# Second MLP, first wide chunk: second layer in seven products, residual rows parked in DRAM, g applied at PSUM

## Chip, cores and metric

The kernel runs on one NeuronCore of a Trainium2 chip. The metric is device time in microseconds (us) of one launch, as the median of several runs. One execution was also taken by the hardware profiler; all rows below come from it.

## What is computed

Attention with a window of 128 keys, a first MLP over tokens and channels ("moe"), and a second MLP ("moe2"); the change touches the second MLP:

```python
def _moe2_ref(x, g_ln, w_ch1, w_ch2):          # x: 4 x 576 x 512, w_ch1: 512 x 2048, w_ch2: 2048 x 512
    mu = np.mean(x, axis=-1, keepdims=True)
    var = np.mean((x - mu) ** 2, axis=-1, keepdims=True)
    xn = (x - mu) / np.sqrt(var + 1e-06) * g_ln
    ch = np.maximum(xn @ w_ch1, 0.0) @ w_ch2
    return (x + ch).astype(np.float32)
```

The 4 x 576 tokens are 18 tiles of 128 rows. float32 accuracy comes from splitting each operand in a high and a low float32r part and adding three products (high-high, high-low, low-high).

## The kernel before

Both MLPs run over three chunks of tokens: a wide one (tiles 0 to 7), a small one (tiles 16, 17) and a wide one (tiles 8 to 15). `steps` lists them as (layer, chunk, tiles, n); layer 1 is the second MLP and has n = 0 to 7 in each chunk, a step taking two blocks of 128 of the 2048 hidden columns. The text calls step n of the second MLP's first wide chunk "1a step n", and that of its second wide chunk "1b step n"; the first MLP's chunks are 0a and 0b.

In a wide chunk the first layer (`seven_products`, lines 1138 to 1140) multiplies 2 x 2 blocks in seven products instead of eight, each of 6 matmuls of 512 columns. Its ends go through `relu_to` (969, 971), which writes the hidden tile's high part on ACT and its low part on DVE. The second layer of step n is spread between the first-layer products of step n + 1. In 1a it is `second` (lines 1236 to 1259): for each of the 8 token tiles 6 matmuls of 512 columns (1251 to 1253), and one DVE addition to the residual `u` (1256). In 1b, steps 0 to 6, it is `second_fast` (1261): seven products for each of two pairs of tiles, of 6 matmuls of 256 columns each (1288), with one copy of a bank to another on ACT (1302) and twelve DVE additions of 512 elements a step (1307). This form needs sums of hidden blocks, which `parts_of` makes at the end of the first layer (1194 to 1203, with splits in high and low on ACT at 385 and on POOL or DVE at 403 or 401), and sums of weight blocks t1 to t4. Those are made once, during 1a, by `keep_sums`: per step eight POOL subtractions of 128 columns and two splits; the results go to DRAM as `ds1nh`, `ds1nl`, and `sums_of` reads them in 1b.

Weights arrive as float64 and are converted by five instructions a block (`load_f64`: ACT 449, DVE 452, 454, 456, 464). `stage_w` converts blocks ahead of their use and keeps them in DRAM (`d`), `load_w` reads them back or converts on the spot. `STAGE_RATES` says how many blocks a step stages, and in the attention stage `W_START` and `W_STEP` place conversions. For blocks of the second MLP's first weight, `convert_w` multiplies by the layer norm's gain g (516, POOL or DVE).

The residual `u` is one SBUF tile of 18 x 512 columns. The order of all engines' instructions is made at build time: every operation carries costs and dependencies, and `Plan.order` lists them by need; engines then run their lists in order.

## Time and profile before

| | |
|---|---|
| median of 3 runs | 834.96 us (833.67 to 835.32) |
| profiled execution | 835.53 us |
| its span, first to last instruction | 833.8 us |
| PE busy | 821.5 us, 99% |
| DVE busy | 659.1 us, 79% |
| POOL busy | 466.9 us, 56% |
| ACT busy | 428.5 us, 51% |

The busy share of PE is the share of the span in which some matmul is under way. The stage of interest, 1a, runs from 448.8 to 611.5 us of the span; 1b's steps from 661.5 us.

### The profile page before, as it was taken

The numbers are of one execution on the slowest core, as the hardware profiler recorded it, in microseconds if no ns is written. First come the engines' busy times: TensorE is split into PE (matmuls) and PEld (weight loads), VectorE is DVE, ScalarE is ACT, GpSimd is POOL, SyncE is SP. The second block draws the span as 40 slices with busy tenths as digits, with TensorE's granted clock in tenths as the row PEclk, the third lists the DMA queues.
The fourth block names the chain that finished last, engine by engine and source line by source line (L and its number), as shares of the span: only waits on it lengthen the run. The fifth ranks groups of instructions, "written<-read, shape, count | busy, mean of one in ns | idle before, by whom it ended". The sixth has DMA issues, their size and how long they took to land.

```text
span 833.8 us, 14352 instructions
## 1 busy us (share of the span) xinstructions
PE 821.5 (99%) x4732; PEld 693.4 (83%) x4732; DVE 659.1 (79%) x1379; ACT 428.5 (51%) x1015; POOL 466.9 (56%) x723
## 2 busy tenths in 40 slices
PE   8999999999999999999999999999999999999998
PEld 6777788888888898888888888888889889999996
DVE  5888777978787989987889868989666767777785
ACT  5888677643344535334368333447456634444430
POOL 2785466756354567544248666857533656666640
PEclk9999999999999999999999999999999999999999
DMA  9679645454678899987861544888977663443302
GB/s 328 191 184 306 232 140 191 143 186 144 216 226 297 293 317 322 339 293 240 280 238 54 188 154 139 290 309 300 354 263 237 226 226 130 137 141 116 102 26 101
DMA packets 80474, 179.21 MB, mean 215 GB/s; under 512 B 9104, under 2 KB 10768, under 8 KB 80400
## 3 DMA queue, kind: packets, MB, share of 16 engines
q1 hardware_dynamic: 79920, 176.98, 62.9%
q0 software_dynamic: 480, 1.31, 0.7%
q8 instruction: 37, 0.61, 0.3%
q14 instruction: 37, 0.30, 0.1%
HBM read 138.15 MB, written 38.80 MB: 212 GB/s over the span
## 4 chain that ended last, share of the span: by engine, by line
PE 92%; DVE 4%; ACT 3%; DMA 1%; issue 1%; POOL 0%; DVEq 0%; ACTq 0%; POOLq 0%
PE tok L1253 10%; PE tok L1251 10%; PE b L1138 10%; PE tok L1252 10%; PE b L1139 10%; PE b L1140 10%; PE tok L1288 5%; PE p L1288 4%; PE ps_s L636 3%; PE ps_v L648 3%; PE p L891 2%; PE b L482 2%; PE b L481 2%; PE b L480 2%; PE ps_t L693 1%; ACT pr L686 1%
## 5 line engine op out<-in xcount | busy, mean ns | idle before, releaser
L1256 DVE TENSOR_TENSOR u<-tok,u 128x512 f32<-128x512 f32 x196 | 134.4, 687 | 52.5 <-PE tok L1253 51.1
L1251 PE MATMUL tok<-w2h,hh 128*128 128x512 f32 x392 | 154.0, 393 | 0.0
L1253 PE MATMUL tok<-w2h,hl 128*128 128x512 f32 x392 | 152.9, 390 | 0.2 <-DVE hl L971 0.2
L1252 PE MATMUL tok<-w2l,hh 128*128 128x512 f32 x392 | 152.8, 390 | 0.0
L1138 PE MATMUL b<-xh,w1h 128*128 128x512 f32 x384 | 150.4, 392 | 0.3 <-DVE b L401 0.3
L1139 PE MATMUL b<-xl,w1h 128*128 128x512 f32 x384 | 149.8, 390 | 0.0
L1140 PE MATMUL b<-xh,w1l 128*128 128x512 f32 x384 | 149.6, 389 | 0.0
L403 POOL TENSOR_TENSOR w1l<-w,w1h 128x256 fp32r<-128x256 f32 (+1 forms) x112 | 78.9, 726 | 111.4 <-ACT w1h L385 103.4
L969 ACT ACTIVATE hh<-b 128x512 fp32r<-128x512 f32 (+1 forms) x112 | 58.7, 542 | 136.8 <-PE b L1140 95.5
L1253 PEld LDWEIGHTS tok<-w2h,hl 128*128 128x128 f32 x392 | 73.6, 188 | 16.4 <-DVE hl L971 0.8
L1251 PEld LDWEIGHTS tok<-w2h,hh 128*128 128x128 f32 x392 | 73.7, 188 | 15.1 <-DVE u L1256 0.8
L971 DVE SCALAR_TENSOR_TENSOR hl<-b,hh 128x512 fp32r<-128x512 f32 (+1 forms) x112 | 67.2, 617 | 23.9 <-ACT hh L969 23.2
L1252 PEld LDWEIGHTS tok<-w2l,hh 128*128 128x128 f32 x392 | 73.7, 188 | 14.3
L1140 PEld LDWEIGHTS b<-xh,w1l 128*128 128x128 f32 x384 | 72.1, 188 | 15.4
L1138 PEld LDWEIGHTS b<-xh,w1h 128*128 128x128 f32 x384 | 72.2, 188 | 14.6 <-DVE b L401 0.7
L1139 PEld LDWEIGHTS b<-xl,w1h 128*128 128x128 f32 x384 | 72.2, 188 | 13.5
L449 ACT ACTIVATE e<-rh 128x512 bf16<-128x512 bf16 (+2 forms) x62 | 39.7, 641 | 69.4 <-DMA rh<-wb 22.2
L403 POOL TENSOR_TENSOR w1l<-st,w1h 128x256 fp32r<-128x256 f32 x58 | 44.9, 795 | 47.9 <-ACT w1h L385 42.0
L686 ACT ACTIVATE pr<-t,mn 128x128 f32<-128x128 f32 x144 | 55.8, 391 | 14.1 <-DVE mn L677 14.0
L704 POOL TENSOR_SCALAR_AFFINE_SELECT pf<-pf 128x512 f32<-128x512 f32 x64 | 42.1, 659 | 34.6 <-ACT pf L385 28.3
L401 DVE TENSOR_TENSOR b<-b,p 128x512 f32<-128x512 f32 x56 | 38.9, 695 | 20.1 <-PE b L1140 19.5
L403 POOL TENSOR_TENSOR xl<-st,xh 128x256 fp32r<-128x256 f32 x48 | 39.0, 834 | 21.0 <-ACT xh L385 16.6
(193 smaller groups left out, 1919.9 us busy)
## 6 DMA issues: line engine op xcount, KB each, us to landing
w<-d SPq DMA_DIRECT2D x86, 256.0 KB, 4.2
rw<-wb SPq DMA_DIRECT2D x32, 512.0 KB, 5.4
rh<-wb SPq DMA_DIRECT2D x32, 512.0 KB, 5.2
rw<-wa SPq DMA_DIRECT2D x24, 512.0 KB, 4.3
rh<-wa SPq DMA_DIRECT2D x24, 512.0 KB, 4.3
d<-y SPq DMA_DIRECT2D x30, 256.0 KB, 5.3
keys<-kT SPq DMA_DIRECT2D x18, 256.0 KB, 4.6
q<-qT SPq DMA_DIRECT2D x18, 256.0 KB, 4.9
```

Of the source, the lines that this page charges most:

```text
L403: ENGINE[e].tensor_tensor(get()[:, c], ga()[:, c], gb()[:, c], alu)
L686: op({"ACT": 580}, lambda m=m: nc.scalar.activation(out=pr.t[:, m], in_=t.t[:, m], func=AF.Exp, bias=mn.t[:, m:m + 1], scale=-1.0, accum_o ...
L969: op({"ACT": act(n, True)}, lambda: nc.scalar.activation(out=hh.t[:, c], in_=go(), func=AF.Relu), [o], [(hh, key)])
L971: mark[0] = op({"DVE": dve(n)}, lambda: nc.vector.scalar_tensor_tensor(out=hl.t[:, c], in0=go(), scalar=0.0, in1=hh.t[:, c].bitcast(F32), ...
L1138: nc.tensor.matmul(g.t, wh.t[:, w], xh.t, start=start and k == 0, stop=False, skip_group_check=True)
L1139: nc.tensor.matmul(g.t, wh.t[:, w], xl.t, start=False, stop=False, skip_group_check=True)
L1140: nc.tensor.matmul(g.t, wl.t[:, w], xh.t, start=False, stop=stop and k == 1, skip_group_check=True)
L1251: nc.tensor.matmul(o.t, hh.t[:, c:c + P], wh.t, start=j == 0, stop=False)
L1252: nc.tensor.matmul(o.t, hh.t[:, c:c + P], wl.t, start=False, stop=False)
L1253: nc.tensor.matmul(o.t, hl.t[:, c:c + P], wh.t, start=False, stop=j == 1)
L1256: op({"DVE": dve(DM)}, lambda o=o, i=i: nc.vector.tensor_tensor(u[i].t, o.t, u[i].t, ALU.add), [o], [u[i]])
L1288: nc.tensor.matmul(o.t[:, p], x()[:, c], y(), start=start and p == 0 and k == 0, stop=stop and p == 1 and k == 2, skip_group_check=True)
```

## The change

1. `FAST2` now also names 1a, steps 1 to 6: their second layer runs as `second_fast`, their first layer ends in `parts_of`.
2. The sums t1 to t4 are needed in the step that makes them. `keep_sums` writes them into new row buffers: raw sums in `f` (one buffer), high and low parts in `r` (four). They still go to DRAM for 1b. Step 0 keeps the old places (`few`).
3. To make room, `u` becomes nine pairs of tiles. The pairs of tiles 8 to 17 live in the buffers `r` and `f`; `put_away` writes them to DRAM when 1a begins (10 DMAs of 256 KB), and `bring_back` reads them at 1a step 7 (10 more). All layer norm statistics of tiles 8 to 15 are now due ahead of that.
4. g is no longer multiplied into the weights. The second MLP's transposed inputs are scaled as they leave PSUM: on ACT by a per-partition scale, on DVE by `scalar_tensor_tensor` in place of `tensor_tensor`.
5. Conversions: from n = 22 on the attention stage has one at every n instead of every second; 0a stages one block a step (before none), 0b three (before two).

```diff
-STAGE_RATES = {(0, 2): 2, (1, 0): 2}
+STAGE_RATES = {(0, 0): 1, (0, 2): 3, (1, 0): 2}
+RESTING, SUMS = range(8, 18), 8
-FAST2 = ((1, 2),)
+FAST2 = {(1, 2): range(7), (1, 0): range(1, 7)}
...
+def pair_of_rows(j):
+    if j == SUMS:
+        pairs[j] = buf("rows", [P, 2, DM], F32, "f", 1)
+    elif 2 * j in RESTING:
+        pairs[j] = buf("rows", [P, 2, DM], F32, "r", len(RESTING) // 2 - 1)
+    else:
+        pairs[j] = buf("big", [P, 2, DM], F32, "u", (NTILE - len(RESTING)) // 2)
+    u[2 * j:2 * j + 2] = [Part(pairs[j], lambda t, k=k: t[:, k]) for k in range(2)]
...
-                if W_START <= n < 2 * NTILE - 4 and (n - W_START) % W_STEP == 0:
+                if W_START <= n < 2 * NTILE - 4 and ((n - W_START) % W_STEP == 0 or n >= W_DENSE):
...
+    def copy_x(dst, get, b, gb, f):
+        if f is None:
+            return copy(dst, get, b, gb, CW, ("ACT",), True)
+        op({"ACT": act(CW, True, 1)}, lambda: nc.scalar.activation(
+            out=get(), in_=gb(), func=AF.Copy, scale=g_sb.t[:, f]), [b, g_sb], [dst])
+    def less(dst, get, b, gb, a, ga, f):
+        if f is None:
+            return minus(dst, get, b, gb, a, ga, CW, ("DVE",))
+        op({"DVE": dve(CW)}, lambda: nc.vector.scalar_tensor_tensor(
+            out=get(), in0=gb(), scalar=g_sb.t[:, f], in1=ga(), op0=ALU.mult, op1=ALU.subtract), [b, g_sb, a], [dst])
...
-        if c == 0 and (layer, 2) in FAST2 and n < (NF1, NF2)[layer] // 2 - 1:
-            keep_sums(layer, n, wtiles[used[0] - 2:used[0]], last)
-        return sums_of(layer, n, out) if fast2(s) else out
+        if c == 0:
+            if n not in FAST2.get((layer, 2), ()):
+                return out
+            places = in_rows() if fast2(s) else in_few()
+            full = in_sums() if fast2(s) else None
+            keep_sums(layer, n, wtiles[used[0] - 2:used[0]], last, *places, full)
+            return with_sums(out, *quarters(*places)) if fast2(s) else out
+        return with_sums(out, *sums_of(layer, n)) if fast2(s) else out
...
+    def put_away(tiles):
+        for i in tiles:
+            d = resting[i] = buf("dram", [P, DM], F32, f"r{i}")
+            op({"DMA": 728}, lambda x=u[i], d=d: nc.sync.dma_start(out=d.t, in_=x.t), [u[i]], [d])
+    def bring_back(tiles):
+        for i in tiles:
+            if i % 2 == 0:
+                pair_of_rows(i // 2)
+            op({"DMA": 728}, lambda x=u[i], d=resting[i]: nc.sync.dma_start(out=x.t, in_=d.t), [resting[i]], [u[i]])
...
+            if (layer, c) == (1, 0):
+                while todo:
+                    do_next()
+                put_away(RESTING)
+        if (layer, c) == (1, 0) and n == NF2 // 2 - 1:
+            bring_back(RESTING)
```

How the built order moves, at three places. PE in 1a, where the second layer of step 1 begins: `b` is a first-layer product, `tok` and `p` are second-layer banks. Before:

```order
L1138 MATMUL b_6281<-xh_5835,w1h 128x512
L1139 MATMUL b_6281<-xl_5846,w1h 128x512
L1140 MATMUL b_6281<-xh_5835,w1l 128x512
L1251 MATMUL tok<-w2h,hh 128x512
L1252 MATMUL tok<-w2l,hh 128x512
L1253 MATMUL tok<-w2h,hl 128x512
```

Now:

```order
L1356 MATMUL tok<-w2h,hl 128x256
L1368 MATMUL p_6357<-hh 128x512
L1206 MATMUL b_6360<-xh_5559,w1h 128x512
L1207 MATMUL b_6360<-xl_5573,w1h 128x512
L1208 MATMUL b_6360<-xh_5559,w1l 128x512
L1206 MATMUL b_6360<-xh_5831,w1h 128x512
L1207 MATMUL b_6360<-xl_5837,w1h 128x512
L1208 MATMUL b_6360<-xh_5831,w1l 128x512
L1356 MATMUL tok<-r,fewh 128x256 x2
L1356 MATMUL tok<-r,fewl 128x256
```

A step's 48 second-layer matmuls of 512 columns are 84 of 256; some of them read the sums in `r` that POOL has just made, and line 1368 is one extra matmul that opens a bank (two in all of 1a).

DVE in the same stretch: additions to the residual, `hl` the hidden low parts, `s`, `m`, `y` the conversion of weights. Before:

```order
L1256 TENSOR_TENSOR u<-tok,u 128x512 x2
L401 TENSOR_TENSOR b_2516<-b_2448,p_6309 128x512
L1256 TENSOR_TENSOR u<-tok,u 128x512 x2
L401 TENSOR_TENSOR b_6281<-b_2448,p_6309 128x512
L1256 TENSOR_TENSOR u<-tok,u 128x512
L401 TENSOR_TENSOR st<-w 128x256
L1256 TENSOR_TENSOR u<-tok,u 128x512
```

Now:

```order
L1266 SCALAR_TENSOR_TENSOR hl<-b_6360,hh 128x512
L1376 TENSOR_TENSOR u<-tok,u 128x2x256
L467 TENSOR_SCALAR s<-e 128x256
L1421 TENSOR_TENSOR rstd<-r_6279,y 128x8
L469 SCALAR_TENSOR_TENSOR s<-e,s 128x256
L416 TENSOR_TENSOR b_2534<-b_2465,p_6483 128x512
L479 SCALAR_TENSOR_TENSOR y<-m,s 128x512
L1376 TENSOR_TENSOR u<-tok,u 128x2x256
L1376 TENSOR_TENSOR u<-p_6357,u 128x2x256
L467 TENSOR_SCALAR s<-e 128x256
L416 TENSOR_TENSOR b_6456<-b_2465,p_6483 128x512
L1376 TENSOR_TENSOR u<-p_6392,u 128x2x256
```

Twelve additions a step stand where eight stood, between conversions and first-layer sums. In the whole order DVE has 72 additions of line 1376 more and 48 of line 1324 (1256 before) fewer; 24 hidden low parts of `relu_to` give way to 18 + 18 instructions of `parts_of`, and DVE takes 9 more low parts `hl<-st`, `fewl<-st` and 2 more sums `st<-st`. POOL takes 30 more halves of such low parts and 8 of such sums.

SP, which issues the DMAs, around the end of 1a step 6: `w` is a weight block, `ds` sums for 1b, `r_...` a parked residual tile. Before:

```order
L1114 DMA rw<-ds10h 128x1024
L1114 DMA rh<-ds10l 128x1024
L1114 DMA rw<-ds11h 128x1024
L1114 DMA y<-ds11l 128x512 x2
L1096 DMA ds16l<-fewh 128x512 x2
L524 DMA d_7523<-w 128x512
L1096 DMA ds16h<-fewl 128x512 x2
```

Now:

```order
L1179 DMA rw<-ds10h 128x1024
L1179 DMA rh<-ds10l 128x1024
L528 DMA d_7773<-y 128x512
L1133 DMA r<-r_5890 128x512
L1133 DMA r<-r_5922 128x512
L1133 DMA r<-r_5953 128x512
L1133 DMA r<-r_5986 128x512
L1161 DMA ds16h<-r 128x512
L1161 DMA ds16l<-r 128x512
L1161 DMA ds16h<-r 128x512
L1133 DMA f<-r_4797 128x512
L1133 DMA f<-r_4802 128x512
```

Ten returns like these stand in the queue; the first four wait until step 5's sums have been used, and the writes of step 6's sums and the next weight loads stand behind them.

## Rows read from the trace of the kernel before

**Rows 1.** The page: busy us (share of span) and instructions by engine.
```profile
PE 821.5 (99%) x4732; PEld 693.4 (83%) x4732; DVE 659.1 (79%) x1379; ACT 428.5 (51%) x1015; POOL 466.9 (56%) x723
```
**Rows 2.** Windows of 1a steps 2 to 6: busy us (instructions) by engine, clock, DMA.
```profile
core 0: us, PE busy (x) PEld busy (x) DVE busy (x) ACT busy (x) POOL busy (x), PEclk, DMA share, GB/s
...
487.60:508.00 20.40, 20.40 (x92) 16.89 (x91) 12.59 (x20) 7.53 (x14) 12.03 (x20) 1.00 0.37 123
508.00:528.60 20.60, 20.60 (x92) 16.84 (x91) 17.61 (x29) 9.19 (x17) 18.74 (x28) 1.00 0.61 204
528.60:549.40 20.80, 20.64 (x91) 16.78 (x90) 19.64 (x31) 8.90 (x17) 17.99 (x28) 1.00 0.89 322
549.40:569.80 20.40, 20.40 (x91) 16.89 (x90) 17.91 (x29) 8.07 (x15) 10.01 (x15) 1.00 0.81 283
569.80:590.20 20.40, 20.40 (x91) 16.89 (x90) 17.90 (x30) 14.71 (x32) 16.33 (x24) 1.00 0.90 295
```
**Rows 3.** The same view: all of 1a, small chunk after it, four steps of 1b.
```profile
448.80:611.50 162.70, 162.54 (x721) 134.02 (x722) 133.59 (x223) 74.76 (x146) 109.26 (x165) 1.00 0.67 230
611.50:661.50 50.00, 50.00 (x327) 45.56 (x327) 32.30 (x57) 32.04 (x72) 21.46 (x30) 1.00 0.79 267
701.20:779.50 78.30, 78.30 (x506) 71.23 (x505) 58.88 (x93) 36.62 (x68) 51.27 (x81) 1.00 0.40 129
```
**Rows 4.** Timeline of PE at a step's border in 1b: start us, length us.
```profile
700.93 0.28 PE L1288 MATMUL tok<-w2l,hh 128*128 128x256 f32 x1
701.05 0.28 PE L1288 MATMUL tok<-w2h,hl 128*128 128x256 f32 x1
701.17 0.40 PE L1138 MATMUL b<-xh,w1h 128*128 128x512 f32 x1
701.40 0.40 PE L1139 MATMUL b<-xl,w1h 128*128 128x512 f32 x1
```
**Rows 5.** Timeline of PE in 1a step 4, around its wait.
```profile
531.96 0.39 PE L1251 MATMUL tok<-w2h,hh 128*128 128x512 f32 x1
532.19 0.39 PE L1252 MATMUL tok<-w2l,hh 128*128 128x512 f32 x1
532.73 0.50 PE L1253 MATMUL tok<-w2h,hl 128*128 128x512 f32 x1 [0.16 <-DVE hl L971]
```
**Rows 6.** Timeline of DVE in the same step.
```profile
542.06 1.05 DVE L464 SCALAR_TENSOR_TENSOR y<-m,s 128x512 f32<-128x512 uint32 x1
543.03 0.68 DVE L1256 TENSOR_TENSOR u<-tok,u 128x512 f32<-128x512 f32 x1
543.64 0.41 DVE L456 TENSOR_SCALAR m<-rw 128x512 uint32<-128x512 uint32 x1
```
**Rows 7.** Groups by form, DVE in 1a: busy us, mean ns; idle before.
```profile
L1256 DVE TENSOR_TENSOR u<-tok,u 128x512 f32<-128x512 f32 x64 | 43.8, 686 | 15.7 <-PE tok L1253 15.3
L464 DVE SCALAR_TENSOR_TENSOR y<-m,s 128x512 f32<-128x512 uint32 x12 | 11.4, 949 | 1.0 <-POOL w L516 0.9
L456 DVE TENSOR_SCALAR m<-rw 128x512 uint32<-128x512 uint32 x11 | 7.4, 676 | 0.0
L516 DVE TENSOR_TENSOR w<-y,g_sb 128x512 f32<-128x512 f32 x3 | 3.2, 1083 | 0.0
```
**Rows 8.** Groups by form, POOL in 1a and (second row) in 1b.
```profile
L516 POOL TENSOR_TENSOR w<-y,g_sb 128x512 f32<-128x512 f32 x3 | 3.7, 1247 | 0.0
...
L403 POOL TENSOR_TENSOR fewl<-st,fewh 128x256 fp32r<-128x256 f32 x26 | 18.7, 752 | 3.7 <-PE tok L1288 3.0 <-ACT fewh L385 0.7
```
**Rows 9.** Windows of 0b: its first step, and all of it.
```profile
319.30:340.70 21.40, 21.08 (x94) 16.89 (x93) 20.50 (x38) 10.13 (x18) 17.82 (x28) 1.00 0.97 346
...
319.30:448.80 129.50, 129.18 (x584) 106.26 (x582) 111.05 (x204) 62.61 (x127) 64.54 (x101) 1.00 0.78 267
```
**Rows 10.** Groups by form, DVE in 0b.
```profile
L464 DVE SCALAR_TENSOR_TENSOR y<-m,s 128x512 f32<-128x512 uint32 x16 | 11.2, 702 | 0.2
L456 DVE TENSOR_SCALAR m<-rw 128x512 uint32<-128x512 uint32 x16 | 8.8, 553 | 0.8 <-DMA rw<-wb 0.7
```
**Rows 11.** DMA of 1a steps 6 and 7 (569.8 to 611.5): totals, one issue line.
```profile
DMA packets 6000, 12.34 MB, mean 296 GB/s; under 512 B 672, under 2 KB 672, under 8 KB 5997
...
q1 hardware_dynamic: 5997, 12.30, 85.2%
...
w<-d SPq DMA_DIRECT2D x12, 256.0 KB, 4.2
```
**Rows 12.** Waits in 1a: who waited for whom, us in total, times, longest.
```profile
ACT w2h L385 <- DMA w<-d: 16.5, 6, 5.8
```

More of the change, by code (lines that the diff above doesn't have):

```diff
@@ L113, in __init__ @@
         self.plan, self.pool, self.spec = whole.plan, whole.pool, whole.spec
-        self.ops, self.track, self.after, self.behind, self.first = [], {}, [], None, set()
+        self.ops, self.track, self.after, self.behind, self.first = [], {}, whole.after, whole.behind, set()
         self.whole, self.get = whole, get
@@ L170, in op @@
                     behind.add(b.behind.ops[0])
-                assert not getattr(b, "closed", False), f"{b.spec[2]} is used after its place was given away"
+                assert not getattr(getattr(b, "whole", b), "closed", False), f"{b.spec[2]} is used after its place was given away"
                 assert write or any(w for key2, (w, _) in b.track.items() if key is None or key2 in (None, key)), \
@@ L350, in open_pool @@
         pl.pools[name] = tc.alloc_tile_pool(name=name, **{"bufs": 1, **kw})
-    for name in ("const", "big", "wa", "raw", "cvt", "small", "hid"):
+    for name in ("const", "big", "rows", "wa", "raw", "cvt", "small", "hid"):
         open_pool(name)
@@ L372, in block_kernel @@
     after = buf("const", [P, P], F32, "after")
-    u_all = buf("big", [P, NTILE, DM], F32, "u")
-    u = [Part(u_all, lambda t, i=i: t[:, i]) for i in range(NTILE)]
+    pairs, u = [None] * (NTILE // 2), [None] * NTILE
+    def pair_of_rows(j):
[6 more added lines that the diff above has]
+        u[2 * j:2 * j + 2] = [Part(pairs[j], lambda t, k=k: t[:, k]) for k in range(2)]
+    for j in range(NTILE // 2):
+        pair_of_rows(j)
     def load(dst, get, nbytes, src):
@@ L877, in turned @@
         b = buf("psm", [P, CW], F32, f"p{turn[0]}")
-        get = [lambda i=i, k=k: u[i].t[:, k * P:(k + 1) * P] for i, k in places]
+        get = [lambda x=u[i], k=k: x.t[:, k * P:(k + 1) * P] for i, k in places]
         xs = [u[i] for i, _ in places]
@@ L1034, in fast2 @@
         layer, c, _, n = steps[s]
-        return (layer, c) in FAST2 and n < (NF1, NF2)[layer] // 2 - 1
+        return n in FAST2.get((layer, c), ())
     def w2_of(s):
@@ L1060, in keep_sums @@
+    def keep_sums(layer, n, w, last, lo, hi, full=None):
         x0, x1 = w
-        places = few()
         d = {p: buf("dram", [P, 2 * DM], F32, f"ds{layer}{n}{p}") for p in "hl"}
-        def all_of(k):
-            return places[0], lambda: places[0].t.bitcast(F32)[:, k, :DM]
+        if full is None:
+            full = [(x, lambda get=get: get().bitcast(F32)) for x, get in lo]
         def part(c):
-            return (places[0], c // 2), lambda: places[0].t.bitcast(F32)[:, c // 2, c % 2 * HW:(c % 2 + 1) * HW]
+            (x, k), get = full[c // 2]
+            return (x, k), lambda: get()[:, c % 2 * HW:(c % 2 + 1) * HW]
@@ L1454, in block_kernel @@
         pl.emit()
-    for n in ("mlq", "mlr", "mlp", "even", "psc", "pst", "psm", "hid", "small", "cvt", "raw", "wa", "big", "const", "dram"):
+    for n in ("mlq", "mlr", "mlp", "even", "psc", "pst", "psm", "hid", "small", "cvt", "raw", "wa", "rows", "big", "const", "dram"):
         pl.pools[n].release()
```

133 lines of the change are left out of this document (77 added, 56 removed).

## The prediction

> **What bounds the kernel now.** I read the page first: PE is busy 99% of the span, DVE 79%, POOL 56% [rows 1]. So time is PE's instruction stream, and the change has to shorten that stream without making PE wait. Then the stage, by windows of single steps. A plain step of 1a takes 20.40 us, two of the five shown 0.20 and 0.40 more [rows 2]. Four steps of 1b, whose second layer already is in seven products, take 78.30 us, 19.58 each [rows 3], with borders at the first product of each step [rows 4]. In neither is PE the only loaded engine: DVE is busy 12.6 to 19.6 us of a plain step and POOL 10.0 to 18.7 [rows 2]; all of 1a is 162.70 us, with DVE 133.59 (82%) and POOL 109.26 (67%) [rows 3]. Where DVE reached 94% of a step, PE waited once for it: the start to start distance of 0.23 us became 0.54 [rows 5]. That is how a loss looks here.
>
> **PE.** 1a steps 1 to 6 get the second layer of 1b, so the expected gain is that of a step's length, 20.40 - 19.58 = 0.82 us, six times: 4.9 us. Each of the two pairs of banks must be opened once by a matmul of 512 columns, 2 x 0.23 = 0.5 us (the distance in [rows 5]), so 4.4. The 0.2 and 0.4 us that two steps lose now [rows 2] belong to an order of DVE work that is written anew; I count them as gone, which makes PE's own floor 162.7 - 4.4 - 0.6 = 157.7 us for 1a, a gain of 5.0.
>
> On the price of narrow matmuls, the Trainium skill ("TensorE: Matmul & The Clock Gate", Back-to-back issue gap) says that spacing is set by weight load and matmul together, about 81 ns at 128 columns and 131 at 512. Halfway between, 84 narrow matmuls would cost more than 48 wide ones and the change would lose by itself. The trace differs: 0.12 us at 256 columns [rows 4] against 0.23 at 512 [rows 5], so I keep the step lengths.
>
> **DVE.** From the built order: 72 additions more and 48 fewer; 36 instructions of `parts_of` for 24 of `relu_to`; 11 more low parts and sums. That is 47 instructions of 512 elements more. When they follow each other, one starts 0.61 us after the other (543.03 to 543.64); standing alone one lasts 0.68 [rows 6, 7]. So 28.7 to 32.0 us more. The multiplications by g leave: three on DVE in 1a, 3.2 us [rows 7]. DVE's need in 1a is then 133.6 + 28.7 - 3.2 = 159.1 us, up to 162.4; the other way, 64 additions that today mostly wait for PE (15.3 us of such waits, [rows 7]) close up from 0.68 to 0.61, some 4.5 us less, 154.6. I take 158, nearest to the first: DVE was not short of work in the dense steps. Against a PE floor of 157.7 this is 100%: the cover under which these additions lie in 1b (DVE 58.88 of 78.30, 75%, [rows 3]) is not there in 1a, because 1a also converts weights and splits the second layer's.
>
> **POOL.** 30 more halves of low parts at 0.75 and 8 of sums at about the same, 28.5 us, less 3.7 of multiplications by g [rows 8]: 109.3 + 24.8 = 134 us, 85% of the stage. The sums t1 to t4 were for 1b and had time; now the matmuls of the next step read them, so POOL's list has a deadline each step, and everything queued behind a late sum (low parts of w1 and w2, of the hidden tiles) is late with it.
>
> **ACT** gets copies of banks, two relus instead of one, and more splits; it stands at 74.76 of 162.70 us [rows 3], so 44 instructions more by the built order, even at 0.68 us each, are 30 us and leave it a third free. Nothing on the path. The g scaling at PSUM keeps the number of instructions on ACT and DVE in the wide chunks; the small one has four halves for two wholes each. Nothing, covered by 50 us in which DVE is busy 32 [rows 3].
>
> **Parking.** The 10 stores fall in 1a's first steps, where the DMA share is low (0.37 in step 2, [rows 2]): free. The statistics that must be ready first were due in the same two steps anyway. The 10 returns are 2.6 MB in steps 6 and 7, which move 12.34 MB at an 85% share [rows 11]; the total would need 103%, so transfers slip by a few us. Who feels it: weight blocks of the same queue, for which ACT waits 16.5 us in 1a already without PE noticing [rows 12]. I take 0, and up to 2 us if one such block is late by its longest wait today, 5.8.
>
> **Conversions earlier.** By the built order each stage keeps about its number of converted blocks; ten more of them go through DRAM rather than being converted in place, with 16 more reloads in all. 0b's first step loses 0.9 us today with DVE at 20.50 of 21.40 and DMA at 0.97 [rows 9]. I take 0, with 0.8 either way, that loss being the bound.
>
> **The sum.** In a stage where DVE's need equals PE's floor, each of the six fast steps and the one behind them loses something. Today's prices of such steps are 0.2 and 0.4 us with DVE at 85 and 94% [rows 2] and 0.9 to 1.0 at 96% [rows 9]. Seven steps at 0.35 are 2.4 us. So 1a ends 5.0 - 2.4 = 2.6 us earlier. The profiled execution's 835.53 us becomes 832.9; the median lies 0.6 below it, 834.96 - 2.6 = 832.4. One plain sentence on the measure: 0.2%, or 1.7 us, is about what can be told from no change.
>
> **Rivals.**
>
> *Full cover.* The planner places conversions where DVE is free and both engines close up to 154.6 us; PE never waits: -5.0, 829.9 us. For it: 1b loses nothing with DVE at 75%, and plain steps at 88% lose nothing either (17.90 of 20.40, [rows 2]). Against: 98% is above every step that lost nothing. Chance 0.16.
>
> *Even.* DVE and POOL set the pace, each step loses 0.7 and the stage ends where it did: 834 to 836 us, say 834.9. For it: the three loads are within 15% of each other and engines run their lists in order, so any one's lateness is the others'. Chance 0.24.
>
> *DVE and POOL in each other's way: slower.* One conversion's last instruction takes 949 ns in 1a and 702 in 0b, its `m<-rw` 676 and 553 [rows 7, 10], while POOL is busy 67% and 50% of these stages [rows 3, 9]. That is 0.37 us a conversion for 17 points of POOL. POOL goes to 85%, again 18 points: 11 conversions x 0.37 = 4 us, and as much again for the other DVE instructions that read two SBUF operands. DVE's need rises from 158 to 166 us; with no loss besides, the stage ends 3 us later than today's 162.7: 838 us. It decides from the point where the slowing exceeds 162.7 - 158 = 4.7 us. Against: 36 of the 47 new DVE instructions read one operand from PSUM. Chance 0.17.
>
> The Trainium skill ("SBUF — State Buffer", Who interferes with whom) calls DVE's second port pair and GpSimd's one lock, held for a whole instruction; it holds for DVE instructions with two SBUF inputs. The 949 against 702 ns agrees, and additions from PSUM show no such spread: 686 ns in 1a [rows 7].
>
> *The returns.* The first four returns wait in SP's list for the last use of step 5's sums, and step 6's sums and weights are behind them. If that use is late, the weights for the small chunk are too: 5.8 us less what the stage has left, about +1.5 net, 836.5 to 837. Chance 0.05.
>
> The change does what it says (the built order has 13 steps of the narrow form where there were 7), so that is no case.
>
> **How the numbers follow.** The forecast (1 to 4.5 us less) has 0.38. Faster by over 0.2%: nine tenths of the forecast and the full cover, 0.34 + 0.16 = 0.50. Slower: the last two rivals and a twelfth of Even, 0.17 + 0.05 + 0.02 = 0.24. Same: what is left of the forecast and of Even, 0.04 + 0.22 = 0.26. The range runs from full cover with a little of 0b's loss, 829.5, to the slower rival, 838.0.
>
> **What would show it.** After the change, 1a steps 2 to 6 of 19.6 us with DVE under 90%: full cover. Steps of 19.8 to 20.2 with single waits of PE for DVE (`u`, `b`) or POOL (`r`, `fewl`): the forecast. Steps over 20.4, `y<-m,s` over 1.1 us: the slower rival. PE waiting for `r` while POOL has stood ready would break the POOL step; a stage 0a to 0b changed by more than 1 us, the step on conversions; new waits at 1a step 7 or the small chunk, the one on the returns.

## The result, and the profile after

The changed kernel takes **843.61 us** (median of 4 runs, 840.74 to 844.0), the kernel before 834.32 us (4 runs, 833.45 to 835.32): ratio 1.0106, 95% interval 1.0083 to 1.0129. It is slower by 9.3 us where 2.6 less were forecast, and beyond the range's upper end of 838.0. The two profiled executions show 7.8 us of it, 843.37 (span 841.4) against 835.53 (span 833.8), since that of before lies above its median.

Where the span's 7.6 us went, by the first product of each stage:

| stage | before, us | after, us |
|---|---|---|
| attention, to the first product of 0a | 159.2 | 161.4 |
| 0a | 124.5 | 124.6 |
| first small chunk and 0b | 165.1 | 165.1 |
| 1a | 162.8 | 168.2 |
| from the second small chunk to the last product | 218.2 | 218.2 |

So two stages got longer: attention lost 2.2 us, 1a lost 5.4 where 2.6 were to be won. One shift over a border hides in the table: four transposes of 128 columns (matmuls with `ident`) moved from 0b into step 0 of 1a, 0.7 us of PE's work, so that step 0 takes 19.1 us where it took 18.4 and PE is busy throughout both. The page's line on engines, beside [rows 1], shows the new instructions and little else:

```profile
PE 821.1 (98%) x4950; PEld 701.2 (83%) x4950; DVE 683.6 (81%) x1426; ACT 454.6 (54%) x1059; POOL 487.2 (58%) x746
```

The windows of 1a, steps 0 to 7 and then the sum, answer to [rows 2, 3] (busy us of each engine and instructions, granted clock, DMA share, GB/s):

```profile
451.10:470.20 19.10, 19.06 (x87) 15.37 (x86) 18.23 (x33) 10.95 (x22) 12.72 (x20) 1.00 0.59 188
470.20:491.60 21.40, 21.40 (x99) 17.82 (x98) 18.54 (x40) 10.93 (x21) 13.21 (x20) 1.00 0.74 251
491.60:510.70 19.10, 19.10 (x122) 17.27 (x121) 18.63 (x32) 11.85 (x23) 18.74 (x27) 1.00 0.71 240
510.70:531.30 20.60, 19.87 (x129) 17.70 (x128) 20.11 (x31) 11.73 (x23) 19.80 (x29) 1.00 0.86 284
531.30:551.40 20.10, 19.89 (x129) 17.88 (x128) 19.96 (x32) 11.81 (x22) 19.54 (x29) 1.00 0.46 162
551.40:571.60 20.20, 19.84 (x129) 17.87 (x128) 19.76 (x34) 12.10 (x22) 19.98 (x28) 1.00 0.77 260
571.60:598.20 26.60, 23.99 (x135) 21.06 (x134) 23.60 (x37) 13.91 (x25) 25.83 (x40) 0.87 0.85 281
598.20:619.30 21.10, 20.14 (x130) 17.95 (x129) 18.77 (x31) 15.01 (x33) 13.78 (x20) 1.00 0.87 301
...
sum 168.20, PE 163.28 PEld 142.91 DVE 157.60 ACT 98.29 POOL 143.59; mean PE 20.41 PEld 17.86 DVE 19.70 ACT 12.29 POOL 17.95
```

In steps 3 to 5 DVE is busy 98 to 99% of a step and POOL 96 to 99%, in step 6 POOL still 97%. Steps 3 to 5 pay half a microsecond to one each, and step 6 pays for all: 26.6 us.

**Attention.** POOL's timeline shows the cause: an instruction of 0.23 us, the new sign row (`g_sb<-g_sb`, the first four columns times -1), waits 4.95 us for the load of g. It was in no term of the prediction. Behind it in POOL's list stand `rc`, `wt1l` and `xl`, and PE's next rows wait for that `xl`:

```profile
23.79 0.23 POOL L863 TENSOR_SCALAR g_sb<-g_sb 128x4 f32<-128x4 f32 x1 [4.95 <-DMA g_sb<-g]
...
24.42 0.87 POOL L418 TENSOR_TENSOR wt1l<-y,wt1h 128x128 fp32r<-128x128 f32 x2
25.24 1.50 POOL L418 TENSOR_TENSOR xl<-u,xh 128x256 fp32r<-128x256 f32 x2
...
26.80 0.50 PE L496 MATMUL tok<-xl,wt1h 128*128 128x512 f32 x1 [2.89 <-POOL xl L418]
```

**Step 6 of 1a.** ACT's, DVE's and PE's timelines, read together, show one late sum going through three lists. POOL comes to the second layer's temporary `st<-st` at 570.78, since low parts of weights and sums stand before it and POOL has had no gap:

```profile
569.20 1.62 POOL L418 TENSOR_TENSOR w2l<-w,w2h 128x256 fp32r<-128x256 f32 x2
570.78 2.12 POOL L418 TENSOR_TENSOR st<-st 128x256 f32<-128x256 f32 x2
...
572.94 0.64 ACT L400 ACTIVATE hh<-st 128x512 fp32r<-128x512 f32 x1 [2.43 <-POOL st L418]
573.48 0.65 ACT L464 ACTIVATE e<-rh 128x512 bf16<-128x512 bf16 x1
574.03 0.58 ACT L1262 ACTIVATE hh<-b 128x512 fp32r<-128x512 f32 x1
574.50 0.59 ACT L1370 ACTIVATE p<-tok 128x512 f32<-128x512 f32 x1
```

ACT's `hh<-st` waits 2.43 us for it and holds, in its list, a conversion and the copy of a bank (`p<-tok`) for which PE stands. DVE waits 0.70 for the same `hh`, and has then three instructions of the conversion (`s<-e`, `m<-rw`, `s<-e,s`, 1.7 us from start to end) before `hl<-b`:

```profile
573.61 1.24 DVE L416 TENSOR_TENSOR hl<-st,hh 128x512 fp32r<-128x512 f32 x1 [0.70 <-ACT hh L400]
...
576.42 0.68 DVE L1266 SCALAR_TENSOR_TENSOR hl<-b,hh 128x512 fp32r<-128x512 f32 x1
...
575.15 0.50 PE L1356 MATMUL p<-r,hh 128*128 128x256 f32 x2 [1.30 <-ACT p L1370]
577.16 0.39 PE L1356 MATMUL tok<-w2h,hl 128*128 128x256 f32 x1 [0.80 <-DVE hl L1266]
578.43 0.80 PE L1206 MATMUL b<-xh,w1h 128*128 128x512 f32 x1 [0.51 <-ACT b L400]
```

PE waits 1.30, 0.80 and 0.51 us within 5 us. Then its granted clock, 1.00 up to here, stands at 0.50 (1.2 of 2.4 GHz). Windows of 2 us:

```profile
574.00:576.00 2.00, 0.85 (x7) 0.85 (x8) 2.00 (x4) 1.10 (x3) 2.00 (x4) 1.00 0.76 234
576.00:578.00 2.00, 1.12 (x8) 0.68 (x6) 2.00 (x4) 0.84 (x2) 2.00 (x4) 0.93 0.88 229
578.00:580.00 2.00, 1.57 (x4) 1.29 (x5) 1.24 (x2) 0.91 (x2) 2.00 (x5) 0.50 0.78 180
...
584.00:586.00 2.00, 2.00 (x9) 1.53 (x9) 2.00 (x4) 0.94 (x3) 2.00 (x3) 0.86 0.97 338
```

### The profile page after: what moved, and what is told of

It reads as the page before. It is cut to its first block, busy times and chain, and to the rows that moved or that the text cites. A ratio compares the mean times of both kernels' runs of the same rounds, so it can differ in the third digit from the quotient of the medians.

```text
span 841.4 us, 15013 instructions
## 1 busy us (share of the span) xinstructions
PE 821.1 (98%) x4950; PEld 701.2 (83%) x4950; DVE 683.6 (81%) x1426; ACT 454.6 (54%) x1059; POOL 487.2 (58%) x746
## 4 chain that ended last, share of the span: by engine, by line
PE 83%; DVE 7%; DMA 4%; POOL 2%; issue 1%; ACT 1%; SPq 0%; DVEq 0%; ACTq 0%; POOLq 0%
PE b L1206 9%; PE b L1207 9%; PE b L1208 9%; PE tok L1319 8%; PE tok L1321 8%; PE tok L1320 8%; PE tok L1356 6%; PE p L1356 5%; PE ps_v L652 3%; PE ps_s L640 3%; PE p L898 2%; PE b L497 2%; PE b L496 2%; PE b L495 2%; PE ps_t L697 1%
## 5 line engine op out<-in xcount | busy, mean ns | idle before, releaser
L1319 PE MATMUL tok<-w2h,hh 128*128 128x512 f32 x296 | 116.7, 394 | 0.0
L1321 PE MATMUL tok<-w2h,hl 128*128 128x512 f32 x296 | 115.5, 390 | 0.0
L1320 PE MATMUL tok<-w2l,hh 128*128 128x512 f32 x296 | 115.5, 390 | 0.0
L1009 ACT ACTIVATE hh<-b 128x512 fp32r<-128x512 f32 (+1 forms) x88 | 44.8, 529 | 100.5 <-PE b L1208 69.2
L1011 DVE SCALAR_TENSOR_TENSOR hl<-b,hh 128x512 fp32r<-128x512 f32 (+1 forms) x88 | 51.5, 599 | 18.5 <-ACT hh L1009 18.0
L1321 PEld LDWEIGHTS tok<-w2h,hl 128*128 128x128 f32 x296 | 55.6, 188 | 12.3 <-DVE hl L1011 0.4
L1319 PEld LDWEIGHTS tok<-w2h,hh 128*128 128x128 f32 x296 | 55.7, 188 | 10.6
L1320 PEld LDWEIGHTS tok<-w2l,hh 128*128 128x128 f32 x296 | 55.7, 188 | 10.4
L708 POOL TENSOR_SCALAR_AFFINE_SELECT pf<-pf 128x512 f32<-128x512 f32 x64 | 42.8, 670 | 33.7 <-ACT pf L400 27.8
L1324 DVE TENSOR_TENSOR u<-tok,u 128x512 f32<-128x512 f32 x64 | 43.8, 688 | 14.0 <-PE tok L1321 13.1
L1324 DVE TENSOR_TENSOR r<-tok,r 128x512 f32<-128x512 f32 x56 | 38.5, 688 | 14.7 <-PE tok L1321 14.2
```

The source lines that it names most:

```text
L1009: op({"ACT": act(n, True)}, lambda: nc.scalar.activation(out=hh.t[:, c], in_=go(), func=AF.Relu), [o], [(hh, key)])
L1011: mark[0] = op({"DVE": dve(n)}, lambda: nc.vector.scalar_tensor_tensor(out=hl.t[:, c], in0=go(), scalar=0.0, in1=hh.t[:, c].bitcast(F32), ...
L1319: nc.tensor.matmul(o.t, hh.t[:, c:c + P], wh.t, start=j == 0, stop=False)
L1320: nc.tensor.matmul(o.t, hh.t[:, c:c + P], wl.t, start=False, stop=False)
L1321: nc.tensor.matmul(o.t, hl.t[:, c:c + P], wh.t, start=False, stop=j == 1)
L1324: op({"DVE": dve(DM)}, lambda o=o, x=u[i]: nc.vector.tensor_tensor(x.t, o.t, x.t, ALU.add), [o], [u[i]])
```

## The experiments

The theory from the traces has two parts. In attention, the sign row alone costs the 2.2 us. In 1a, POOL's and DVE's in-order lists are both full, and work that PE needs soon stands behind work that it needs later. Rivals: DVE is slowed by POOL (the prediction's slower rival), the parking and the returns of the residual rows cost it, or the clock does. Each kernel is the changed one with the edit shown.

**The sign row later.** It moves to iteration 20 of attention; no other instruction moves.

```diff
                 if n == 1:
                     load_bias(2, 4)
                     load(g_sb, lambda: g_sb.t[:, :4].rearrange("p k o -> p (k o)"), P * DM // P * 4, g)
-                    op({"POOL": 200}, lambda: nc.gpsimd.tensor_scalar(g_sb.t[:, 4:], g_sb.t[:, :4], -1.0, None, ALU.mult), [], [g_sb])
+                if n == 20:
+                    op({"POOL": 200}, lambda: nc.gpsimd.tensor_scalar(g_sb.t[:, 4:], g_sb.t[:, :4], -1.0, None, ALU.mult), [], [g_sb], [len(pl.ops) - 1])
```

> The changed kernel, but the one new POOL instruction of the attention stage, the negation of g (g_sb<-g_sb), stands later in POOL's list, behind the softmax of a later tile; every other instruction of every engine stands where it stood. Theory: in the changed kernel POOL waited 4.95 us at that instruction for the load of g, the low part xl behind it came late and PE lost 2.9 us of wait (3.4 us from start to start), so that the first MLP began at 161.4 us of the span where it had begun at 159.2. Moved, the first MLP begins at 159.0 to 159.6 and the run takes about 841.4 us (2.2 less than 843.6). Rival: the attention stage is longer because other instructions were reordered there, and the wait only shows up at this place; then it begins at 161 or later and the run stays at 843 to 844.

Measured: 840.3 us (ratio to before 1.0071, 1.0056 to 1.0086), 3.3 less than the changed kernel; the first MLP begins at 158.9 and POOL's `xl` at 23.89. Attention's whole length differs by some us from run to run, as do the clock and the loads of its first 20 us (granted 0.83 to 1.00 there in all the profiles here), so the local row is the better witness: PE's busy time from 20 to 40 us. The kernels before, after, and this one:

```profile
20.00:40.00 20.00, 19.50 (x190) 15.69 (x189) 17.81 (x79) 16.95 (x66) 14.95 (x28) 1.00 0.65 209
...
20.00:40.00 20.00, 16.90 (x158) 13.58 (x156) 15.29 (x58) 13.05 (x51) 12.33 (x23) 0.91 0.52 172
...
20.00:40.00 20.00, 19.46 (x193) 15.48 (x190) 17.78 (x79) 16.93 (x66) 15.00 (x27) 1.00 0.66 202
```

In all eleven profiles with the sign row late it is 19.46 to 19.60, in the four with it early 16.67 to 18.86. The whole agrees: attention and 0a together take 285.4 to 287.5 us in the four, and 281.9 to 285.0 in the six with it late in which nothing else ahead of 1a is changed. That the sign row is the cause in attention is settled; its price is less so. The same edit on the kernel without seven products in 1a also gives 3.3 us of the median (840.09 to 836.76, both below). But the changed kernel's one execution with a mean granted clock of 0.998 took 840.74 us, 0.2 to 0.6 more than three of this kernel at that clock, and its three at 0.993 to 0.996 took 843.4 to 844.0; how much of the clock they lost because of the sign row is not shown.

1a stays at 168.1 us, although here the clock is 1.00 throughout: the halved clock is not what the chunk lost. Step 6 then takes 24.8 and step 7 22.8, in sum 47.6, as the changed kernel's 47.7.

**No seven products in 1a**, all else kept (sign row early).

```diff
-FAST2 = {(1, 2): range(7), (1, 0): range(1, 7)}
+FAST2 = {(1, 2): range(7), (1, 0): ()}
```

> The changed kernel with the second layer of 1a's steps 1 to 6 as before (eight products); the parking of rows, g at PSUM and the moved conversions stay. Theory (POOL's and DVE's lists are full in 1a because of parts_of, the early sums and the narrow additions): 1a takes about 162.7 us as before, no PE wait over 0.5 us in it, and the run is 843.6 - 5.5 = 838 us; the 2.2 us in attention and up to 1 us in 0b stay. Rival (the returns of the parked rows and the fuller DMA queues of 1a are what is late): 1a stays at 166 us or more, with waits at its steps 6 and 7, and the run is over 841.

Measured: 840.09 us (1.0081, 1.0059 to 1.0103); 1a 163.9 us, against 162.8 before. So the seven products cost 4.3 us in 1a. The 1.1 over the kernel before are the four transposes in step 0, 0.7, and one wait of PE for DVE in step 2, 0.4. I had expected 162.7 and 838 us: 1a is nearer to that than to the rival. The run lies between, nearer to the rival's 841: 1a is 1.2 us longer than expected, and the median lies 0.9 above the profiled run. What follows 1a takes 218.2 us as before. The returns are not it.

```profile
451.30:615.20 163.90, 163.39 (x725) 134.22 (x725) 130.26 (x226) 75.34 (x150) 99.97 (x156) 1.00 0.74 261
```

**POOL made lighter** (in steps 2 to 6 each subtraction for the sums t1 to t4 runs over 16 of its 128 columns, so that the sums are not computed; their one buffer `f` is kept instead of taken anew each step), and **DVE made lighter** (eight of the twelve additions a step run over 32 of their 512 elements, so that the residual is not computed), each alone. Every list keeps its order. The first edit, in its main part, and the second:

```diff
+            if n > 1 and full[0][0][0] is not lo[0][0][0]:
...
+                    for k in (slice(0, 16), slice(HW // 2, HW // 2 + 16)):
+                        nc.gpsimd.tensor_tensor(get()[:, k], ga()[:, k], gb()[:, k], ALU.subtract)
```

> The changed kernel with POOL's eight subtractions a step for the sums t1 to t4 narrowed from 128 to 16 columns in 1a's steps 2 to 6 (the sums are then not computed); all lists keep their order, DVE, ACT, PE and DMA have the same work. POOL loses some 3.5 us of work a step. Theory that POOL's list is what is late: step 6 falls from 26.6 us to under 21.5, PE keeps its full clock, 1a falls from 168.2 to 160 to 162.5 us and the run to 836 to 838. Rival that DVE's list is what is late (DVE was busy 19.8 of 20.2 us in step 5): POOL gets idle time but step 6 stays over 24 us and the run over 841.

```diff
             c = slice(half * HW, (half + 1) * HW)
+            n = 16 if steps[s][1] == 0 and half else HW
+            c = slice(half * HW, half * HW + n)
...
-                x.t[:, :, c], o.t, x.t[:, :, c], ALU.add), [o, u[i], u[i + 1]], [u[i], u[i + 1]])
+                x.t[:, :, c], o.t[:, :, :n], x.t[:, :, c], ALU.add), [o, u[i], u[i + 1]], [u[i], u[i + 1]])
```

> The changed kernel with eight of DVE's twelve additions to the residual in a narrow second layer of 1a narrowed from 512 to 32 elements (the other columns of these are left out); all lists keep their order, POOL has the same work. DVE loses some 3.5 to 4 us of work a step. Theory that POOL's list is what is late: PE's waits in steps 3 to 6 shrink little, step 6 stays over 23 us, 1a at 165 us or more, the run over 841. Rival that DVE's is: step 6 under 21.5, 1a at 160 to 162.5 and the run at 836 to 838. If both gain half, the two hold each other up (they share work on the same chains, or slow each other's instructions).

Measured: 839.28 (1.0065, 1.005 to 1.008) and 840.39 us (1.0078, 1.0062 to 1.0095). All of 1a in the first and in the second, and step 6 of each:

```profile
452.50:616.60 164.10, 160.72 (x944) 140.57 (x943) 156.09 (x264) 98.55 (x188) 133.74 (x207) 1.00 0.74 255
572.10:595.00 22.90, 21.27 (x135) 18.66 (x134) 22.12 (x37) 13.43 (x25) 21.45 (x37) 1.00 0.91 324
...
450.50:616.10 165.60, 161.47 (x944) 141.56 (x942) 137.96 (x263) 98.11 (x188) 142.99 (x207) 0.99 0.75 253
569.30:594.10 24.80, 22.56 (x135) 19.77 (x134) 19.62 (x37) 14.02 (x25) 24.80 (x38) 0.93 0.88 298
```

Ten us of POOL taken away give 4.1, twenty of DVE give 2.6, and step 6 stays late in both. Neither list alone is the bound. With POOL light neither set of my figures came out: 1a takes 164.1 where the theory had 160 to 162.5, step 6 22.9 where it had under 21.5 and the rival over 24. With DVE light 1a and step 6 came out as the theory that POOL is late had them (165 or more, over 23); the run, 840.4, is just under its 841.

**Both, with the sign row late.**

> The sign row of g is computed late (as in e1), and in steps 2 to 6 of the second MLP's first wide chunk both reliefs are made at once: the subtractions of the weight sums on POOL are narrowed to 16 columns (the sums are not computed) and eight of twelve additions a step on DVE run over 32 elements instead of 512 (the residual is not computed there). Theory (POOL's and DVE's lists are both full, each holds the other up, and nothing else is late): steps 2 to 6 take 19.0 to 20.3 us, the first wide chunk 158 to 161 us, step 6 no longer stands out, the clock stays full there, and the run is 830 to 834 us. Rival (the order inside the lists at step 6, with ACT's list held by hh<-st, is late whatever the load): step 6 stays at 22 us or more, the chunk at 162 us or more, the run at 835 us or more.

Measured: 833.18 us (0.9992, 0.998 to 1.0005), 1a 162.0. The two reliefs nearly add up (4.1 + 2.6 against 6.1), steps 3 to 5 take 19.6 to 19.7, but step 6 still takes 22.1. All of 1a, and step 6:

```profile
447.20:609.20 162.00, 160.19 (x944) 140.65 (x943) 133.94 (x264) 98.48 (x188) 133.71 (x207) 1.00 0.74 257
565.80:587.90 22.10, 21.20 (x134) 18.65 (x133) 18.15 (x37) 13.34 (x24) 21.37 (x37) 1.00 0.91 333
```

Chunk and step 6 came out as the rival had them, the run as the theory had it: full lists explain steps 3 to 5. Step 6 needs something more, the order or the work that POOL still has in this step: POOL is busy 97% of it, and PE's own length of the step is 20.3 (next experiment).

**Conversions.** The diff is against the kernel of the first experiment; two conversions a step in 0a leave seven in 1a instead of eleven (not five, as I expected), the last at 560.6 instead of 587.3 us, ahead of step 6.

```diff
-STAGE_RATES = {(0, 0): 1, (0, 2): 3, (1, 0): 2}
+STAGE_RATES = {(0, 0): 2, (0, 2): 3, (1, 0): 2}
```

> Everything is computed. The sign row late as in e1, and two weight conversions a step instead of one in the first MLP's first wide chunk, so that six fewer stand in the second MLP's first wide chunk (about 2.1 us of DVE and 0.67 us of ACT each there, so 13 us of DVE). Theory (DVE's list is one of the two that are full): the second MLP's first wide chunk takes 162 to 165.5 us instead of 168.1, the first MLP's first wide chunk 124.6 to 125.6, the run 835 to 838 us. Rival (POOL alone decides; DVE's relief in e4 came from the additions being away, not from DVE's time): the chunk stays at 167 us or more and the run at 840 us or more.

> As e5 (sign row late; the weight sums' subtractions narrowed on POOL, so that they are not computed; eight of twelve additions a step narrowed on DVE, so that the residual is not computed there), and two conversions a step in the first MLP's first wide chunk, so that six fewer stand in the second MLP's. Theory (step 6 is late because conversions stand in front of the hidden layer's splits in DVE's and ACT's lists): step 6 takes 20.0 to 20.6 us instead of 22.1, and the second MLP's first wide chunk 158.5 to 160.5 us instead of 162.0; the run 831 to 833.5 us, since the first MLP then takes 1 to 1.5 us more, as in e6. Rival (step 6 waits on the ring of temporaries or on PSUM banks, whatever stands in the lists): step 6 stays above 21.5 us and the chunk at 161.5 us or more.

The second is that same edit on top of both reliefs. Measured: 838.91 (1.0051, 1.0034 to 1.0068) and 836.41 us (1.0023, 1.0009 to 1.0037). In 1a the edit alone gives 6.1 us, as much as both reliefs, so that 1a takes 162.0 us, the best figure of its theory, and step 6 20.3. With both reliefs 1a takes 159.4 and PE waits nowhere in it, as expected too, so that steps 3 to 6 show PE's own length, 19.6 to 19.7 and in step 6, which holds six matmuls more, 20.3. Step 6 and all of 1a with the edit alone, then steps 3, 6 and all of 1a with all three:

```profile
571.50:591.80 20.30, 20.30 (x134) 18.54 (x133) 19.98 (x32) 11.76 (x22) 19.58 (x32) 1.00 0.49 163
...
451.40:613.40 162.00, 159.55 (x944) 140.43 (x942) 152.98 (x254) 96.29 (x184) 134.65 (x196) 1.00 0.70 237
...
510.30:530.00 19.70, 19.70 (x128) 17.88 (x127) 17.39 (x33) 13.41 (x25) 17.62 (x30) 1.00 0.70 219
...
569.20:589.50 20.30, 20.30 (x134) 18.54 (x133) 16.32 (x31) 11.50 (x22) 18.51 (x33) 1.00 0.50 160
...
450.70:610.10 159.40, 158.80 (x944) 140.44 (x942) 131.04 (x253) 96.43 (x184) 125.53 (x198) 1.00 0.72 239
```

So it is load and order together: PE's lists are fed in time with DVE at 82% and POOL at 79% of 1a, not with DVE at 94% and POOL at 85%; and step 6 goes free when no conversion stands in it any more. The edit does two things there, however. It also takes 9.3 us of work off POOL in 1a (143.99 to 134.65), nearly as much as the POOL relief, since the planner gives low parts of weights back to DVE; of POOL's instructions in step 6, 37, it leaves 32. That POOL's total load is not the whole cause is shown by the kernel with both reliefs: POOL's work in 1a is as small there (133.71), DVE's is smaller, and step 6 is late. Whether the conversions' own instructions or the low parts moved with them free step 6 is not separated. The DMA share of step 6 falls too, from 0.91 to 0.49; in the kernel before it is 0.90 in step 6 [rows 2] and nothing is lost.

But the runs are longer than expected, since the 6.1 us were not kept. Attention and 0a together take 287.0 us instead of 283.6, and what follows 1a 219.1 instead of 218.2. Of these, 0a's 126.8 instead of 124.7 is no loss in 0a: PE never waits there, and nine matmuls of 512 columns that stood ahead of its first product now stand behind it. The time is lost in attention: the two runs with this edit, 287.0 and 286.3, lie above the 281.9 to 285.0 named above. Why is open. The run with all three reliefs, 836.41, is slower than with two.

**How many seven-product steps** (all computed, sign row late): three alternate, none, five, three at the start, one of the last four lines in each.

```diff
-FAST2 = {(1, 2): range(7), (1, 0): range(1, 7)}
+FAST2 = {(1, 2): range(7), (1, 0): (1, 3, 5)}
+FAST2 = {(1, 2): range(7), (1, 0): ()}
+FAST2 = {(1, 2): range(7), (1, 0): range(1, 6)}
+FAST2 = {(1, 2): range(7), (1, 0): range(1, 4)}
```

> Everything is computed. The sign row late as in e1, and only steps 1, 3 and 5 of the second MLP's first wide chunk run their second layer in seven products. Theory (the load adds up over neighbouring steps, and a plain step after each fast one lets POOL and DVE catch up): TensorE's gain is three times 0.8 = 2.5 us, the parking costs 1 us, so the chunk takes 160 to 162.5 us and the run 832 to 835 us. Rival (each seven-product step makes its own wait, whatever stands beside it): the three steps take over 21 us each, the chunk 164 us or more, the run 836 us or more.

> Everything is computed. The sign row late as in e1, and no seven-product step in the second MLP's first wide chunk: what is left of the change is the parking of ten tiles, the scaling by g at PSUM and the conversions spread. Theory (the attention loss is the sign row alone, and parking with the rest costs 1.1 us): first MLP begins at 158.9 us, the chunk takes 163.5 to 164.3 us, the run is 835 to 837.5 us, 0 to 0.4 percent over the kernel before. Rival (parking and the spread conversions cost nothing, the 1.1 us in e2 was scatter): the chunk at 162.8 us, the run within 1 us of the kernel before.

> Everything is computed. Sign row late; seven products in steps 1 to 5 of the second MLP's first wide chunk, not in step 6. Theory (only the chunk's end is in trouble, where the conversions meet the seven-product steps): 163.5 to 165.5 us for the chunk and 836 to 838.5 us for the run. Rival (the trouble moves with the last seven-product step): the chunk at 166.5 us or more, the run 839 us or more.

> Everything is computed. Sign row late; seven products in steps 1 to 3 only. Theory (the seven-product steps before the conversions lose at most 1 us each, a little over the 0.8 us that each gains on TensorE): the chunk 162.5 to 164 us, near e8's 163.5, the run 836 to 837.5 us. Rival (the steps gain as predicted as long as they are early in the chunk): the chunk 160.5 to 162 us, the run 834 to 835.5 us. Other rival (each costs, as e7's): the chunk 165 us or more, the run 838 us or more.

| steps in seven products | none | 1 to 3 | 1, 3, 5 | 1 to 5 | 1 to 6 |
|---|---|---|---|---|---|
| 0b and 1a, us (before: 292.2) | 291.6 | 294.1 | 296.5 | 295.4 | 296.2 |
| 1a alone, us | 163.5 | 165.6 | 170.9 | 167.3 | 168.1 |
| run, us | 836.76 | 839.63 | 840.1 | 837.61 | 840.3 |
| ratio, 95% interval | 1.002 to 1.004 | 1.005 to 1.008 | 1.0038 to 1.0071 | 1.0028 to 1.0058 | 1.0056 to 1.0086 |

(Of the alternate order 2.5 us of products moved from 0b into 1a, hence the line with both.) In the columns 1, 3, 5 and 1 to 5, 0.4 us are transposes that otherwise follow 1a. With none, 1a came out at the 163.5 us of the theory, but not for its reason: PE waits 0.1 us in it, and the 0.7 over the kernel before are the four transposes. The other three theories were too good for the chunk, which each time came out as a rival had it (of the runs, only that with five came out as its theory had it, 836 to 838.5): over none, three steps cost 2.5 or 4.9 us where six cost 4.6, and the waits come earlier when the seven-product steps do. With steps 1 to 3 the longest, 0.9 and 0.7 us, stand in PE's steps 3 and 4, where both lists are full again:

```profile
508.50:528.80 20.30, 19.38 (x122) 17.01 (x121) 20.27 (x29) 11.85 (x23) 20.04 (x30) 1.00 0.70 214
528.80:550.40 21.60, 20.87 (x135) 18.55 (x134) 21.01 (x35) 11.92 (x22) 21.60 (x34) 1.00 0.87 311
```

**The rest of attention, and another place for the conversions.** With none in seven products 2.7 us stay over the kernel before, and none of it is a wait in 1a. I put the weight loads of attention back to every second iteration, first without and then with seven products; the second pair has five conversions a step in 0b.

```diff
-WT_SHIFT, WT_START, WT_STEP, SHIFT_AT, W_START, W_STEP, W_DENSE = 0, 2, 1, 7, 12, 2, 22
+WT_SHIFT, WT_START, WT_STEP, SHIFT_AT, W_START, W_STEP, W_DENSE = 0, 2, 1, 7, 12, 2, 99
-STAGE_RATES = {(0, 0): 1, (0, 2): 3, (1, 0): 2}
+STAGE_RATES = {(0, 0): 1, (0, 2): 5, (1, 0): 2}
```

> Everything is computed. As e8 (sign row late, no seven-product step in the second MLP's first wide chunk), and the weight loads during attention again at every second iteration, as in the kernel before, instead of at every one from the 22nd on. Theory (what e8 still loses, 2.7 us, lies mostly in the denser loads of attention): the run is 834 to 835.5 us, the first MLP begins at 158.5 to 159.7 us. Rival (the rest lies behind attention, in the parking and the spread conversions): the run stays at 836 to 837.5 us.

> Everything is computed. Sign row late; five conversions a step instead of three in the first MLP's second wide chunk, so that eight conversions instead of eleven stand in the second MLP's first wide chunk, the last of them about 100 instructions of DVE earlier than before. The first MLP's first wide chunk keeps one a step. Theory (what e6 won, 6 us, came from the conversions that stood beside the seven-product steps, and the two us that e6 paid lay in the place it moved them to): the second MLP's first wide chunk takes 162 to 165 us, the first MLP's small and second wide chunk 165 to 166 us, the run 834.5 to 838 us. Rival (conversions cost the same wherever they go): the sum of these stretches stays at 333 us and the run at 839 us or more.

> Everything is computed. As e13, with the weight loads of attention at every second iteration, as in the kernel before. Theory (the denser loads cost about 1 us, from e9 beside e8): 0.5 to 1.5 us less than e13. Rival (they cost nothing, e9 and e8 differed by scatter): within 0.5 us of e13.

Measured: 835.8 (1.0016, 1.0007 to 1.0026), 845.2 (1.013, 1.0108 to 1.0152) and 840.52 us (1.0069, 1.0047 to 1.0092). The sparse loads give 1.0 us in the first, which lies between the two expectations and whose interval meets that of the kernel with the dense ones, and 4.7 in the last against the one before it, more than I expected. So in the first pair a cost of the dense loads is not shown; in the second it is, and in the profiles 4.4 us lie in attention and 0a (288.6 and 284.2). The executions' mean clock differs there too, 0.991 to 0.996 and 0.996 to 1.000, and by which transfer the loads cost I did not trace. 0b in the last two:

```profile
324.80:456.20 131.40, 129.07 (x581) 105.98 (x579) 111.26 (x211) 63.43 (x127) 64.31 (x105) 1.00 0.82 288
...
320.00:453.20 133.20, 130.72 (x580) 107.01 (x579) 113.97 (x214) 63.60 (x126) 65.28 (x105) 0.99 0.84 292
```

1a falls to 164.4 and 161.9 us as the theory says, and 0b rises from 128.1 to 131.4 and 133.2. Small chunk, 0b and 1a together take 332.0 and 331.0 us, where the kernel with three conversions a step takes 333.1: moving conversions moves most of their price, as the rival (333) had it. The run of 845.2 is longer than either theory had it; its profile has attention at 164.4 us. No kernel here that computes everything is faster than the kernel before; the nearest is 835.8 us.

## Why the prediction was wrong, step by step

- **PE's term held.** A step of seven products was to take 19.58 us; with the lists light they take 19.60 to 19.70, and 1a without any wait of PE 159.4 against the floor of 157.7. Of these 1.7 us, 0.7 are the four transposes.
- **DVE's need held, by two errors that cancel**: 158 was taken, 157.60 are busy, 100% of PE's floor, as said. But DVE got 41 instructions more where 47 less the three by g were counted, as the planner gave low parts of weights to POOL, and its conversions took longer (see the slower rival).
- **POOL's need was too small**: 134 was taken, 143.59 are busy. The price of a half, 0.75, from 1b's low parts (second row of [rows 8]) is the smaller part of that: the 38 new halves cost 0.79 to 0.84 each, 30.1 us where 28.5 were counted. The term that failed is the old work, taken as unchanged. The 48 subtractions for the sums take 27.8 us instead of 24.3, and of low parts and sums of weights POOL has 89 instructions and 63.0 us where it had 80 and 56.0, work that DVE had before. Groups of POOL in 1a after, and one before (count, busy us, mean ns, idle before):

```profile
L418 POOL TENSOR_TENSOR fewl<-st,fewh 128x256 fp32r<-128x256 f32 x18 | 13.8, 788 | 0.0
L418 POOL TENSOR_TENSOR hl<-st,hh 128x256 fp32r<-128x256 f32 x12 | 9.8, 839 | 0.2 <-ACT hh L400 0.2
L418 POOL TENSOR_TENSOR f<-w,f 128x128 f32<-128x128 f32 x24 | 14.8, 635 | 0.0
...
L403 POOL TENSOR_TENSOR fewh<-w,fewh 128x128 f32<-128x128 f32 x24 | 12.4, 537 | 0.0
```

- **The loss in 1a, 2.4 us, was the main failure**: 168.2 less the floor of 157.7 is 10.5, of which 8.8 lie above the 159.4 us in which PE never waits. Its seven prices came from single steps in the 80s and 90s of per cent [rows 2, 9], each followed by steps with room, where a late list catches up. Here steps 3 to 6 have none, so lateness is handed on: 1.0, 0.5, 0.6 us over 19.58 in steps 3 to 5, then 6.3 over the 20.3 of step 6, of which 2.6 are waits of PE and 3.7 slower matmuls, most of them at the halved clock. The sentence on POOL's deadlines named the mechanism; no term carried it.
- **ACT "nothing on the path" failed in step 6**, though its need was bounded rightly (98.29 us busy, at most 105 said). An engine that is idle two fifths of the time delayed PE, because its list stood behind one `hh<-st`.
- **g at PSUM "nothing" failed in attention**: the multiplications in the chunks cost nothing, but the preparation of g's negative, one instruction of 0.23 us ahead of urgent work on POOL, cost 2.2 us of the profile; moving it gave 3.3 of the median. I costed the step by its instructions in 1a and did not look where its setup stands in POOL's list.
- **Parking**: 0 with up to 2 was said, and it held: with plain steps PE waits 0.1 and 0.5 us in 1a (0.2 before). **The returns**: nothing, as said. **Conversions earlier**: 0 with 0.8 either way was said; 0a to 0b take 289.7 against 289.6 us, but with the four transposes gone from 0b, so 0.7 were lost there, within the bound. That the denser loads cost in attention was not in it.
- **The slower rival** had the sign, the steps over 20.4 and a part of the mechanism. Its mark, `y<-m,s` over 1.1 us, is absent: 871 ns, and 949 before [rows 7]. But the kernel before is not the best measure of it. In the two kernels with the sign row late and none or six steps in seven products, POOL is busy 61% and 86% of 1a, and a conversion's four instructions on DVE take 2.22 and 2.62 us in sum. That is 0.40 us a conversion, where the rival had 0.37, and over eleven some 4.4 us of DVE's need. POOL made lighter takes little of it back (2.54). The growth is in `m<-rw` and `s<-e,s`; `y<-m,s` takes 832 and 856 ns. With none, and with six:

```profile
L471 DVE TENSOR_SCALAR m<-rw 128x512 uint32<-128x512 uint32 x11 | 5.5, 504 | 0.1
L469 DVE SCALAR_TENSOR_TENSOR s<-e,s 128x256 int32<-128x256 int32 x12 | 6.5, 544 | 0.1
...
L471 DVE TENSOR_SCALAR m<-rw 128x512 uint32<-128x512 uint32 x11 | 7.8, 712 | 0.0
L469 DVE SCALAR_TENSOR_TENSOR s<-e,s 128x256 int32<-128x256 int32 x12 | 7.8, 646 | 0.0
```

The rule on the shared port that the prediction cites from the Trainium skill ("SBUF — State Buffer", Who interferes with whom), for DVE instructions with two SBUF inputs, is neither borne out nor refuted by this: `s<-e,s` got longer, `y<-m,s` hardly, `w1l<-st,w1h` shorter (1211 to 1042 ns), and `m<-rw`, with one input, grew most. What it would do to POOL's own instructions no run separates.

What stays open: which single conversion or sum would have to stand elsewhere in the lists for step 6 to go free. That the conversions, the sums and the additions each carry part of 1a's loss is shown. In step 6 the additions alone carry nothing that can be seen (24.8 us with and without them at the clocks they had), and the conversions are not separated from the low parts that move with them. A reordered list with the same work was not run, so that the order of the lists makes step 6 is argued from the timelines and not shown.
